# A block-sparse attention feeding a GELU network: shared end-block products moved together, and seven hand-written orders dealt anew

## The chip, the cores and the metric

The kernel runs on one NeuronCore of a Trainium2 chip. The metric is the device time of one execution in microseconds. Three runs of the kernel before took 274.44, 275.01 and 275.5; the median is 275.01. One execution was also recorded by the hardware profiler; every duration, wait and clock in this text comes from that record.

## What is computed

Four batches of eight heads, 768 tokens, 64 numbers a head. Attention looks only at some blocks of 32 tokens: the neighbours, the first and the last block, and three sampled blocks for each of the 24 blocks of queries; the first and the last block of queries see everything. The output, as 3072 tokens of 512 numbers, goes through two matrix products with an exact GELU between.

```python
blk_i, blk_j = pos[:, None] // 32, pos[None, :] // 32
mask = np.abs(blk_i - blk_j) <= 1
mask = mask | (blk_i == 0) | (blk_j == 0) | (blk_i == 23) | (blk_j == 23)
mask[qb * 32:(qb + 1) * 32, kb * 32:(kb + 1) * 32] = True    # three kb for each qb
scores = np.where(mask, np.matmul(q, k.T) / 8, -1e9)
attn = softmax(scores)
x = np.matmul(attn, v)                # (4, 8, 768, 64) -> (3072, 512)
h = x @ w_in                          # 512 -> 2048
out = (0.5 * h * (1 + erf(h / sqrt(2)))) @ w_out
```

## The kernel before

Half a batch is a **unit**: 12 blocks of queries, three *quads* of four. There are eight units; the even ones are *dense* (quads 1, 2, 0) and also do the first and last block of queries of their batch, which see all keys. For each unit the kernel runs FFN1 (first product and GELU, `ffn1_step`, 64 products of 384 columns in eight steps), and then the attention of the *next* unit, with the second product of this unit (FFN2, 48 products of 512 columns) let in between in single pieces by `ffn2_pieces`. Unit 0's attention has nothing to be mixed with but idle products. The attention of unit n is called stage n here; stages 1 to 7 therefore contain FFN2 of the unit before.

The order inside a stage is written by hand as a string of words (`PLANS`, and one string for unit 0), which `attention` (line 600 and on) reads one by one. Each engine executes its instructions in the order in which the words issue them:

- `sN` the score products of round N (`scores`, L346, TensorE, array tile 64x32, into one of two `psA` buffers). A round is two blocks of queries, or one block in the last round of a group of three, or one half of a dense block.
- `mN` its maxima (`maxima`, L372 and L375, VectorE); `eN` its exponentials (L389 and L393, ScalarE), which free the `psA` buffer; `tN` the transpose of 32x32 blocks (L406 and L411, VectorE) into `pT`, which the values products read.
- `wa`, `wb`, `wc` the products with the values for a group (`values`, L470, TensorE); `wd` those of the dense blocks (L433). Groups a and b have four blocks of queries (four *slots*, two rounds each), group c has three. `av` lies in the single `psV` buffer, except for the last group of some units.
- `da`... the division (`divided`, L485 to L489, VectorE); `oa`... the turn to columns (`outputs`, L499, TensorE, with copies on ScalarE), `O` the same with the copy in two parts.
- `fN` N pieces of FFN2 (L566, 128x128 array tile); `S` the pending copy and store of a finished quad (ScalarE, then a store on SP's queue); `G` the load of ScalarE's GELU table.
- `x...` only in stage 1: `xk0` to `xk3` and `xq0` to `xq3` turn one pair of heads of batch 1's keys or queries (`turn_pair`, 16 transposes on TensorE, L234, then one move by ScalarE, or by VectorE with a `d`), `xv` issues the loads of batch 1's values, `xs` repeats the first block of keys.

A slot's values products are eight 32-key chunks c: c = 0 the first block of the sequence, 1 to 3 the neighbours, 4 to 6 the sampled blocks, 7 the last block. Chunks 0 and 7 have the same values for all slots, so for a group with four slots one product with 128 columns of weights serves all four (64x128 array tile, called wide here), where the others take one product with 32 columns for each slot (64x32 tile, narrow). All are done for both heads of a pair (`h`) and both halves of the heads (`G`). The order of the wide products within a group is:

```python
for G in halves:
    work = work + ends if len(halves) == 2 and G else ends + work
```

so a group of four slots issues 4 wide, 48 narrow, 48 narrow and 4 wide products. `start` is set on the first product that writes a slot, for each G anew.

The values of a batch come by eight loads on POOL's queue in the order `VORDER` (`load_values`, L141), heads 0 to 3 first. Keys and queries of batch 1 come by four loads on the same queue behind the weights (`load_kq`, L110), two halves of the heads each; the words `xk` and `xq` use them. Copies of the sampled blocks' keys and values into `gb` (`gather`, L304) run on VectorE and POOL.

Of the kernel before, what the change touches and what calls it, by code (L numbers as in the profile page):

```python
# [20 lines left out]
def kernel(  # L21
# [22 lines left out]
    V2 = 2 * VW  # L44
# [100 lines left out]
    VORDER = sorted(range(H), key=lambda h: (h // 4, (h % 4 ^ h // 4) % 2, h % 4))  # L145
# [273 lines left out]
    def values(unit, grp, halves):  # L419
# [18 lines left out]
        else:  # L438
# [3 lines left out]
            shared = len(slots) == 4  # L442
            for G in halves:
                c0 = KC + V2 * G
                ends = [(0, 4, c, kv[:, blk, c0:c0 + V2]) for c, blk in ((0, 0), (7, NB - 1))] if shared else []
                work = []
                for c in range(1, 7) if shared else range(8):
                    for s, j in enumerate(slots):
# [9 lines left out]
                        work.append((s, 1, c, src))  # L458
                work = work + ends if len(halves) == 2 and G else ends + work
                fresh, left = set(range(len(slots))), {s: 0 for s in range(len(slots))}  # L460
                for s, w, _, _ in work:
                    for x in range(s, s + w):
                        left[x] += 1
                for s, w, c, src in work:
                    at = range(s, s + w)
                    for x in at:
                        left[x] -= 1
                    for h in range(2):
                        rows = slice(64 * h, 64 * h + 64)
                        nc.tensor.matmul(av[32 * s:32 * (s + w), h, V2 * G:V2 * G + V2],  # L470
                                         lhsT=pv[rows, G, c % 4, BL * s:BL * (s + w), c // 4], rhs=src[rows],
                                         start=s in fresh, stop=left[s] == 0)
                    fresh -= set(at)
# [126 lines left out]
    def attention(unit, filler, plan, extra={}, ahead=None):  # L600
# [10 lines left out]
        todo |= {k + c for k in "wdo" for c in groups}  # L611
        for word in plan.split():
            what, arg = word[0], word[1:]
            if what == "s":
                at = [int(i) for i in arg.split("+")]
                scores(rounds[at[0]][0], *[rounds[i][1] for i in at])
                todo -= {f"s{i}" for i in at}
                continue
# [90 lines left out]
    def next_keys(b):  # L709
# [107 lines left out]
```

## Time and profile before

| | us |
|---|---|
| median of three runs | 275.01 |
| the profiled execution | 275.15 |
| its span, first to last instruction | 273.4 |
| TensorE busy | 250.3 |
| VectorE busy | 208.3 |
| ScalarE busy | 206.7 |
| GpSimd busy | 101.7 |

The span is the time between the first and the last recorded instruction; the execution's time has 1.75 us around it. A row of a timeline gives the start, the time until the end of the last of its merged instructions, the engine, the line, what is written from what, the array tile where there is one, and how many instructions were merged; in brackets stands how long the engine had been idle and what released it. Products are pipelined: one of 512 columns lasts 0.38 but the next starts 0.22 after it, and a row may overlap the next one. Some records of products are missing from the trace (an "issue" wait of 0.16 ahead of FFN2 pieces is one such record, not a wait). PEld rows are the weight loads that precede the products.

### The profile page before, as it was taken

The numbers are of one execution on the slowest core, as the hardware profiler recorded it, in microseconds if no ns is written. First come the engines' busy times: TensorE is split into PE (matmuls) and PEld (weight loads), VectorE is DVE, ScalarE is ACT, GpSimd is POOL, SyncE is SP. The second block draws the span as 40 slices with busy tenths as digits, with TensorE's granted clock in tenths as the row PEclk, the third lists the DMA queues.
The fourth block names the chain that finished last, engine by engine and source line by source line (L and its number), as shares of the span: only waits on it lengthen the run. The fifth ranks groups of instructions, "written<-read, shape, count | busy, mean of one in ns | idle before, by whom it ended". The sixth has DMA issues, their size and how long they took to land.

```text
span 273.4 us, 11478 instructions
## 1 busy us (share of the span) xinstructions
PE 250.3 (92%) x4899; PEld 143.7 (53%) x4933; DVE 208.3 (76%) x477; ACT 206.7 (76%) x378; POOL 101.7 (37%) x210
## 2 busy tenths in 40 slices
PE   0798699899999999999999999999999999999995
PEld 0624486355564555545555566455645655465544
DVE  7599969598898989589998987698949996882000
ACT  8679766896868885797868976988788966985611
POOL 7797980717595000950962003910040033000000
PEclk9999689999999999999999999999999999999999
DMA  6999499959999317991997108991101110111002
GB/s 96 183 70 163 75 148 193 206 116 122 63 161 142 102 43 112 114 88 42 120 152 119 62 35 154 89 61 44 40 0 43 43 41 0 38 44 43 0 38 77
DMA packets 73508, 23.80 MB, mean 87 GB/s; under 512 B 63089, under 2 KB 70514, under 8 KB 73458
## 3 DMA queue, kind: packets, MB, share of 16 engines
q0 software_dynamic: 57440, 13.64, 84.4%
q1 hardware_dynamic: 16018, 9.44, 13.6%
q8 instruction: 38, 0.62, 1.0%
q14 instruction: 12, 0.10, 0.1%
HBM read 27.26 MB, written 6.29 MB: 123 GB/s over the span
## 4 chain that ended last, share of the span: by engine, by line
PE 73%; DMA 9%; ACT 6%; DVE 5%; issue 3%; POOL 3%; POOLq 0%; ACTq 0%
PE hp L523 27%; PE op L566 22%; PE av L470 9%; PE sc L346 6%; DMA kn<-in_k_dram 6%; DMA qn<-in_q_dram 3%; PE tx L499 2%; PE op L596 2%; ACT L417 2%; PE pt L234 2%; PE av L433 2%; ACT pp L393 2%; PE av L596 1%; POOL gb L304 1%; ACT pp L389 1%
## 5 line engine op out<-in xcount | busy, mean ns | idle before, releaser
L523 PE MATMUL hp<-xT,w_in_sb 128*128 128x384 bf16 (+2 forms) x536 | 84.9, 319 | 0.2 <-ACT xT L507 0.2
L389 ACT ACTIVATE pp<-sc,nm 128x256 bf16<-128x256 f32 x176 | 74.9, 540 | 7.7 <-DVE nm L372 7.1
L566 PE MATMUL op<-w_out_sb,g 128*128 128x512 bf16 x305 | 75.8, 380 | 4.0 <-issue 3.8
L523 PEld LDWEIGHTS <-w_in_sb 128*128 128x128 bf16 x536 | 51.1, 98 | 33.1 <-issue 0.3
L545 ACT ACTIVATE g<-hp 128x768 bf16<-128x768 f32 x56 | 45.2, 809 | 25.9 <-PE hp L523 25.9
L372 DVE TENSOR_REDUCE nm<-sc 128x4 f32<-128x1024 f32 (+1 forms) x48 | 53.2, 1115 | 6.3 <-PE sc L346 6.0
L566 PEld LDWEIGHTS <-g 128*128 128x128 bf16 x336 | 28.7, 98 | 34.0 <-issue 6.5
L304 POOL COPY gb<-kv 128x388 bf16 (+1 forms) x87 | 36.6, 472 | 23.8 <-DVE gb L295 21.6
L304 DVE COPY gb<-kv 128x388 bf16 x177 | 38.4, 295 | 0.3 <-DVE gb L295 0.2
L406 DVE STREAM_TRANSPOSE pT<-pp 128x512 f32<-128x512 f32 (+1 forms) x48 | 31.4, 657 | 5.3 <-ACT pp L389 4.6
L470 PE MATMUL av<-kv,pT 64*32 64x130 bf16 (+1 forms) x1344 | 30.6, 229 | 1.9 <-DVE pT L406 1.2
L470 PEld LDWEIGHTS <-pT 64*32 64x32 bf16 (+1 forms) x2400 | 26.2, 94 | 10.2 <-DVE pT L406 4.0
L165 POOL COPY mark<-gb 1x1 bf16<-1x1 bf16 x6 | 1.1, 178 | 76.5 <-DVE gb L304 76.5
L141 POOL DMA_DIRECT2D kv<-in_v_dram x32 | 23.0, 726 | 2.5 <-DMA qn<-in_q_dram 1.4
L346 PE MATMUL sc<-gb,qT 64*32 64x256 bf16 x704 | 18.5, 275 | 2.6 <-ACT pp L389 1.8
L507 ACT COPY xT<-tx 128x512 bf16<-128x512 bf16 (+1 forms) x32 | 13.7, 453 | 9.1 <-PE tx L499 9.1
L470 PE MATMUL av<-gb,pT 64*32 64x130 bf16 x1056 | 20.2, 231 | 0.0
L346 PEld LDWEIGHTS <-qT 64*32 64x32 bf16 x832 | 9.3, 90 | 20.4 <-issue 12.3
L417 ACT ACT_TABLE_LOAD x15 | 19.2, 1283 | 0.2
L489 DVE TENSOR_TENSOR xh<-av,rec 128x512 bf16<-128x512 f32 (+2 forms) x28 | 18.2, 652 | 1.0
L393 ACT ACTIVATE pp<-sc,nm 128x768 bf16<-128x768 f32 x16 | 16.7, 1101 | 2.5 <-DVE nm L375 2.2
L550 ACT COPY os<-op 128x512 f32<-128x512 f32 (+1 forms) x23 | 13.1, 570 | 7.0 <-PE op L596 4.3
(79 smaller groups left out, 230.2 us busy)
## 6 DMA issues: line engine op xcount, KB each, us to landing
out_dram<-os SPq DMA_DIRECT2D x23, 256.0 KB, 3.3
kv<-in_v_dram POOLq DMA_DIRECT2D x32, 96.0 KB, 6.6
w_in_sb<-in_moe_w_in_dram POOLq DMA_DIRECT2D x4, 512.0 KB, 7.3
w_out_sb<-in_moe_w_out_dram POOLq DMA_DIRECT2D x2, 1024.0 KB, 12.1
kn<-in_k_dram POOLq DMA_DIRECT2D x4, 384.0 KB, 10.8
qn<-in_q_dram POOLq DMA_DIRECT2D x4, 384.0 KB, 12.2
qn<-in_q_dram POOLq DMA_DIRECT2D x12, 128.0 KB, 5.4
kn<-in_k_dram POOLq DMA_DIRECT2D x12, 128.0 KB, 5.9
```

Source lines behind the costliest of these rows:

```text
L141: nc.gpsimd.dma_start(out=kvs[b % 2][32 * hh:32 * hh + 32, 0:NB, c0:c0 + D], in_=v[b, h].rearrange("(n p) d -> p n d", p=BL))
L304: (engine or nc.vector).tensor_copy(sampled(unit.place[j], r)[:, None, c0:c1], src[:, bass.ds(at[j][r], 1), :])
L346: nc.tensor.matmul(o, lhsT=qT[rows, j // 4, pr, BL * (j % 4):BL * (j % 4) + BL], rhs=rhs(rows, pr), start=True, stop=True)
L372: nc.vector.tensor_reduce(out=nm[:, 0:2 * n].rearrange("p (g j) -> p g j", g=2), in_=A4[:, :, 0:n, :], op=ALU.max, axis=AX.X, negate=True)
L389: nc.scalar.activation(at[:, x // n, x % n], A[:, a:a + 256].rearrange("p (e c k) -> p e c k", e=2, k=BL), AF.Exp, bias=nm[:, x:x + 1])
L393: nc.scalar.activation(pp[:, 0:S].rearrange("p (c k e) -> p c e k", e=2, k=BL), A[:, 0:S].rearrange("p (c e k) -> p c e k", e=2, k=BL), AF ...
L406: nc.vector.transpose(pt.rearrange("p g c x -> p (g c) x")[:, :, 64 * s:64 * (s + n)].bitcast(F32), pp[:, 0:512 * n].bitcast(F32).rearrang ...
L417: nc.scalar.activation(junk, zero[0:1, 0:1], func)
L470: nc.tensor.matmul(av[32 * s:32 * (s + w), h, V2 * G:V2 * G + V2], lhsT=pv[rows, G, c % 4, BL * s:BL * (s + w), c // 4], rhs=src[rows], st ...
L523: nc.tensor.matmul(hp[:, i, c0:c1], lhsT=w_in_sb[:, ki, (m + i) * P:(m + i + 1) * P], rhs=xTs[n % 2][:, ki, c0:c1], start=(ki == 0), stop= ...
L545: nc.scalar.activation(g[:, m:m + 2, 0:T], hp[:, :, 0:T], AF.Gelu)
L566: nc.tensor.matmul(op, lhsT=g[:, m, t * P:(t + 1) * P], rhs=w_out_sb[:, m, :], start=(m == 0), stop=(m == KOUT - 1))
```

## The change

Four things change. The values products of both halves G are collected into one list, the eight wide products of a four-slot group stand together, and they come first, or last where the TensorE word before was a score round or a values block that is not the dense one; `start` is now set once for each slot and not for each half. The heads 4 to 7 of the values are loaded first. In unit 1's order the keys are turned later. The orders of units 2 to 7 are dealt anew.

```diff
-    VORDER = sorted(range(H), key=lambda h: (h // 4, (h % 4 ^ h // 4) % 2, h % 4))
+    VORDER = sorted(range(H), key=lambda h: (-(h // 4), (h % 4 ^ h // 4) % 2, h % 4))
...
-    def values(unit, grp, halves):
+    def values(unit, grp, halves, ends_last=False):
...
+            ends, work = [], []
             for G in halves:
                 c0 = KC + V2 * G
-                ends = [(0, 4, c, kv[:, blk, c0:c0 + V2]) for c, blk in ((0, 0), (7, NB - 1))] if shared else []
-                work = []
+                if shared:
+                    ends += [(G, 0, 4, c, kv[:, blk, c0:c0 + V2]) for c, blk in ((0, 0), (7, NB - 1))]
                 for c in range(1, 7) if shared else range(8):
...
-                        work.append((s, 1, c, src))
-                work = work + ends if len(halves) == 2 and G else ends + work
-                fresh, left = set(range(len(slots))), {s: 0 for s in range(len(slots))}
...
+                        work.append((G, s, 1, c, src))
+            work = work + ends if ends_last else ends + work
+
+            fresh, left = set(range(len(slots))), {s: 0 for s in range(len(slots))}
...
+        tall = False
         for word in plan.split():
             what, arg = word[0], word[1:]
+            if what in "sfwoOx":
+
+                before, tall = tall, what in "sw" and arg[0] != "d"
...
-                values(unit, groups[arg[0]], halves)
+                values(unit, groups[arg[0]], halves, before)
...
     PLANS = {
-        1: ("s0 m0 s1 f12 m1 e0 e1 S xk0d s2 f1 m2 t0 f5 s3 e2 xq0d f5 m3 t1 xk1 t2 e3 s4 m4 f4 xq1 xv wa  "
-            "s5 t3 m5 xk2d f5 e4 s6 f1 da e5 xq2 wb m6 t5 db S xq3 t4 s7 f3 m7 oa f3 xk3d wc f1 e7 e6 ob  "
-            "f4 dc t7 Oc t6 f5 xs G"),
-        2: ("S s1 s0 m1 f3 e1 f6 m0 s2 t1 m2 e0 e2 t0 f7 s3 wd s4 m3 f2 t2 f4 e3 dd m4 od e4 f4 t3 s5 m5  "
-            "wa e5 s6 t4 m6 f6 da f2 s7 m7 e6 e7 S f1 t5 G f5 t6 oa t7 wb wc db f1 dc ob f4 Oc"),
-        3: ("s0 m0 e0 s1 m1 e1 t0 f14 s2 m2 f5 s3 S t1 f2 e2 wa m3 e3 t2 da s5 f3 m5 f4 e5 oa s4 f2 t3 wb  "
-            "m4 f2 e4 t5 f4 db S s6+7 t4 m7 ob wc e7 f8 m6 dc e6 Oc f1 t6 t7 G"),
-        4: ("s0+1 f11 m0 m1 e0 s2 f3 t0 S e1 m2 s3 f2 e2 t1 m3 e3 t2 f1 wd s4 f5 s5 m4 f6 dd f2 e4 t3 m5  "
-            "od s6 wa f1 t4 m6 f1 e5 f1 da s7 e6 m7 f2 e7 t5 f1 t6 oa f4 wb t7 wc f1 G db S ob f4 dc Oc  "
-            "f1"),
-        5: ("s0 m0 s1 m1 e0 f14 e1 t0 s2 f5 m2 s3 f2 t1 m3 f1 wa e2 s5 f4 t2 e3 da S m5 f1 t3 oa s4 m4 f4  "
-            "e5 e4 t5 wb db t4 S f5 s6+7 ob m6 wc f8 e6 m7 dc e7 Oc G f1 t7 t6"),
-        6: ("s0+1 m0 m1 f8 e0 f3 e1 t0 S s2 m2 f3 t1 f1 e2 f3 s3 m3 wd e3 s4 t2 f3 m4 f3 s5 dd f2 m5 f4  "
-            "t3 e4 f1 t4 od s6 wa e5 f2 s7 f2 m6 da f1 m7 t5 f1 e6 f2 t6 f1 e7 t7 oa wb db G wc f1 dc ob  "
-            "f3 S f1 Oc f1"),
-        7: ("s0 m0 e0 s1 f7 m1 e1 f7 t0 s2 m2 f5 t1 s3 m3 f9 e2 t2 S s4 S e3 wa m4 da s5 f4 e4 t3 f6 m5  "
-            "e5 oa t4 t5 wb db wc dc f1 G ob f4 Oc"),
+        1: ("s0 f5 s1 m0 m1 e0 e1 f8 s2 f2 m2 xk0 f1 t0 s3 S f2 xq0d f5 e2 xk1 m3 t1 s4 f3 m4 e3 t3 xq1  "
+            "xv wa s5 da t2 f1 m5 xk2 f5 e4 xq2d wb t4 f2 e5 xq3 db s6 s7 f1 ob f4 S t5 m7 m6 xk3d wc dc  "
+            "e7 e6 oa f2 xs t6 f3 Oc f2 t7 G f3"),
+        2: ("s1 m1 e1 s0 f10 m0 e0 t1 s2 f2 m2 t0 e2 f5 S s3 wd m3 s4 f2 t2 e3 f7 m4 dd e4 s5 t3 od f1 m5  "
+            "wa s6 f2 e5 f6 t4 m6 e6 f1 s7 da m7 t5 f1 t6 S f3 e7 f1 oa t7 wb wc G db ob f4 dc Oc"),
+        3: ("s0 s1 f1 m0 f3 m1 f5 e0 f5 t0 s2 e1 m2 e2 f5 t1 f3 s3 m3 wa da s4 m4 t2 f5 S e3 f1 e4 oa f4  "
+            "t3 s5 m5 e5 wb t4 f4 s6+7 db ob t5 m7 e7 m6 e6 wc f6 dc f2 Oc G t7 S t6 f1"),
+        4: ("s0+1 m0 S m1 e0 f11 s2 e1 t0 f5 m2 e2 s3 t1 m3 e3 t2 f1 wd s4 f5 s5 m4 e4 dd t3 f7 od s6 m5  "
+            "t4 wa e5 m6 da f6 e6 s7 f3 m7 t5 f2 e7 t6 oa G t7 wb wc S db f1 ob f3 dc f1 Oc f1"),
+        5: ("s0 s1 m0 m1 e0 S f14 s2 f1 e1 f4 s3 f3 t0 m2 e2 t1 m3 wa s5 f4 t2 m5 f2 da e3 S t3 s4 e5 oa  "
+            "m4 f4 wb f5 t5 e4 db s6+7 t4 ob m7 m6 wc dc e7 e6 t6 f7 Oc G f1 t7"),
+        6: ("s0+1 S f4 m0 e0 f6 m1 f1 e1 s2 t0 f5 m2 s3 e2 f1 t1 wd m3 s4 t2 e3 f7 m4 e4 s5 dd m5 f6 s6  "
+            "t3 f2 e5 S m6 wa t4 s7 e6 f5 da m7 od e7 f3 t5 t6 oa wb t7 wc db f1 G dc ob f4 Oc f1"),
+        7: ("s0 s1 f9 m0 e0 f1 m1 t0 f5 e1 s2 f4 m2 t1 s3 f8 m3 e2 e3 t2 f1 s4 f1 m4 wa e4 S s5 f5 t3 m5  "
+            "f4 e5 da oa t4 wb G t5 wc db f1 dc ob f4 S Oc"),
     }
```

Unit 0's order is not changed, but its values blocks take the new form: `wa` follows a score round and has its wide products last, `wb` has them first.

More of the change, by code (lines that the diff above doesn't have):

```diff
@@ L457, in values @@
                             src = sampled(unit.place[j], c - 4)[:, c0:c0 + V2]
-                        work.append((s, 1, c, src))
-                work = work + ends if len(halves) == 2 and G else ends + work
-                fresh, left = set(range(len(slots))), {s: 0 for s in range(len(slots))}
[L461 to L473, printed above, removed]
+                        work.append((G, s, 1, c, src))
+            work = work + ends if ends_last else ends + work
+            fresh, left = set(range(len(slots))), {s: 0 for s in range(len(slots))}
+            for G, s, w, _, _ in work:
+                for x in range(s, s + w):
+                    left[x] += 1
+            for G, s, w, c, src in work:
+                at = range(s, s + w)
+                for x in at:
+                    left[x] -= 1
+                for h in range(2):
+                    rows = slice(64 * h, 64 * h + 64)
+                    nc.tensor.matmul(av[32 * s:32 * (s + w), h, V2 * G:V2 * G + V2],
+                                     lhsT=pv[rows, G, c % 4, BL * s:BL * (s + w), c // 4], rhs=src[rows],
+                                     start=s in fresh, stop=left[s] == 0)
+                fresh -= set(at)
             n, m = len(slots), 4
```

## The prediction

> **What bounds the kernel now.** I read the page's busy table first, then busy time by stretch (cut at the FFN1 blocks), then TensorE's waits, then TensorE's timeline in single stages.
>
> ```profile
> span 273.4 us, 11478 instructions
> PE 250.3 (92%) x4899; PEld 143.7 (53%) x4933; DVE 208.3 (76%) x477; ACT 206.7 (76%) x378; POOL 101.7 (37%) x210
> ```
>
> ```profile
> 0.00:38.50 38.50, 26.22 (x688) 15.78 (x691) 30.54 (x70) 30.04 (x47) 33.07 (x89) 0.91 1.67 120
> 48.40:72.20 23.80, 21.80 (x588) 12.31 (x593) 19.32 (x31) 18.85 (x39) 11.85 (x29) 1.00 1.71 134
> 82.70:103.50 20.80, 19.37 (x560) 10.94 (x564) 18.34 (x34) 17.50 (x38) 3.31 (x8) 1.00 0.72 89
> 114.00:131.90 17.90, 17.10 (x461) 9.09 (x466) 15.60 (x25) 15.73 (x34) 8.66 (x16) 1.00 1.83 65
> 142.40:162.20 19.80, 19.00 (x559) 10.54 (x563) 17.49 (x31) 17.44 (x37) 2.89 (x7) 1.00 0.47 79
> 172.70:190.60 17.90, 17.11 (x460) 9.01 (x465) 15.42 (x25) 15.78 (x35) 6.00 (x12) 1.00 1.70 63
> 201.10:221.30 20.20, 19.34 (x559) 10.86 (x563) 17.69 (x31) 17.38 (x38) 0.69 (x2) 1.00 0.08 29
> 231.80:249.00 17.20, 16.52 (x445) 9.21 (x449) 13.17 (x21) 15.01 (x34) 0.00 (x0) 1.00 0.09 34
> ```
>
> Columns: stretch, length, busy us of TensorE (PE), its weight loads, VectorE (DVE), ScalarE (ACT), GpSimd (POOL), granted clock. The first row is unit 0's attention, the others are the attention stages of units 1 to 7, whose orders are rewritten; the FFN1 blocks between them are not touched. In stages 1 to 7 TensorE is busy 92 to 97% of the time, but VectorE and ScalarE are at 77 to 88% as well: two engines stand close behind the one that bounds.
>
> ```profile
> PE sc L346 <- ACT pp L389: 1.8, 3, 0.9
> PE pt L234 <- DMA kn<-in_k_dram: 1.6, 2, 0.9
> PE av L470 <- DVE pT L406: 1.2, 1, 1.2
> PE av L470 <- issue: 0.5, 1, 0.5
> ```
>
> These are nearly all the waits of TensorE behind the start-up. The 0.9 is the key transpose in stage 1; the 1.2 is in unit 0; the 0.5 is a stall inside one values block of stage 2 with no releaser. So TensorE's length in stages 2 to 7 is its own work plus what it loses where it changes from one kind of work to another.
>
> **The hand-overs.** Stage 3, once with FFN2 pieces on both sides, once between two score rounds in stage 2:
>
> ```profile
> 123.98 0.60 PE L566 MATMUL op<-w_out_sb,g 128*128 128x512 bf16 x2
> 124.52 0.58 PE L470 MATMUL av<-kv,pT 64*128 64x130 bf16 x28
> ...
> 125.12 0.42 PE L470 MATMUL av<-kv,pT 64*32 64x130 bf16 x24
> 125.32 0.42 PE L470 MATMUL av<-gb,pT 64*32 64x130 bf16 x24
> 125.67 0.29 PE L470 MATMUL av<-kv,pT 64*128 64x130 bf16 x4
> 125.89 0.55 PEld L566 LDWEIGHTS <-g 128*128 128x128 bf16 x4
> ...
> 92.50 0.41 PE L346 MATMUL sc<-gb,qT 64*32 64x256 bf16 x16
> 92.85 0.58 PE L470 MATMUL av<-kv,pT 64*128 64x130 bf16 x28
> 94.00 0.29 PE L470 MATMUL av<-kv,pT 64*128 64x130 bf16 x4
> 94.22 0.41 PE L346 MATMUL sc<-gb,qT 64*32 64x256 bf16 x16
> ```
>
> 24 narrow products (64x32 array tile) start within 0.20 us. The last 24 begin at 125.32, so they are through at 125.52; the four wide ones (64x128 tile) start at 125.67. That gap, 0.15, is the price of a change of array tile. The block takes 1.37 either way (124.52 to 125.89, 92.85 to 94.22): 0.80 of narrow products, the rest eight wide ones and three hand-overs.
>
> **The change part by part.** *Values.* The same 104 products of a four-slot block run as 8 wide + 96 narrow, or 96 narrow + 8 wide where the last TensorE word was a score round or another values block. One hand-over inside goes, and another where the narrow end meets narrow score rounds or the narrow `wc`. The before shows no score round directly followed by narrow products: bounds 0.01 (same tile, pitch of the narrow products) and 0.15 (as between any two tiles); I take 0.01, since both use the 64x32 tile. The Trainium skill (TensorEngine Tiling, Key Properties) says that a change of tiling mode drains the array, a change of tile within a mode does not; the 0.15 agrees with the first half, no pair here shows the second; by it the 0.01 holds.
>
> Counted from the order strings, stage by stage (1 to 7), changes of array tile: before 29, 20, 20, 22, 20, 21, 16 = 148; after 30, 17, 14, 18, 17, 18, 13 = 127. (With the old orders and new values it would be 123, so the new orders themselves win none.) 21 × 0.15 = 3.15 us of TensorE time; bounds 0 and 3.15.
>
> How much of it arrives depends on VectorE. In unit 3 the new order puts round 4's maxima and both transposes behind the division of group a: da, m4, t2, t3, and then `wb`, which needs t3.
>
> ```profile
> 118.33 1.19 DVE L372 TENSOR_REDUCE nm<-sc 128x4 f32<-128x1024 f32 x1
> 119.44 0.69 DVE L406 STREAM_TRANSPOSE pT<-pp 128x512 f32<-128x512 f32 x1
> 120.05 1.18 DVE L372 TENSOR_REDUCE nm<-sc 128x4 f32<-128x1024 f32 x1
> ...
> 121.95 0.13 DVE L485 TENSOR_SCALAR den<-av 128x8 f32<-128x8 f32 x1
> ...
> 122.95 0.68 DVE L372 TENSOR_REDUCE nm<-sc 128x2 f32<-128x512 f32 x1
> ...
> 114.78 2.97 PE L566 MATMUL op<-w_out_sb,g 128*128 128x512 bf16 x13 [0.16 <-issue]
> ```
>
> Start to start: maximum 1.11, transpose 0.61, division 1.00 (121.95 to 122.95). From the end of `wa`: 1.00 + 1.11 + 0.61 + 0.69 = 3.4, plus 0.1 until the division sees the sums and 0.1 to the products: 3.6. TensorE meanwhile has s4 (0.35), ten FFN2 products at 0.216 ((2.97 − 0.38)/12) = 2.16, oa (0.2), s5 and its hand-overs (0.2): 2.9. So `wb` waits some 0.7, which eats most of that stage's six hand-overs (0.9): −0.2 there. In the other stages I find no such reversal against the order before (units 2 and 7: t3 ahead of m5), but TensorE, being earlier, meets operands that VectorE, at 77 to 88%, delivers no earlier. Of the other 15 hand-overs (2.25) I let a little over half arrive: −1.3. Sum **−1.5**.
>
> *Later keys in unit 1.*
>
> ```profile
> 37.59 15.22 DMA kn<-in_k_dram
> 48.44 0.63 PE L346 MATMUL sc<-gb,qT 64*32 64x256 bf16 x32
> 49.01 2.93 PE L566 MATMUL op<-w_out_sb,g 128*128 128x512 bf16 x11
> 52.86 0.53 PE L234 MATMUL pt<-identity,kn 96*64 96x96 bf16 x16 [0.93 <-DMA kn<-in_k_dram]
> ```
>
> The keys land at 37.59 + 15.22 = 52.81. TensorE was through at 51.94, and could have started 0.16 earlier (a product lasts 0.38, its successor starts after 0.216): lost 1.1. The new order puts 15 FFN2 products ahead instead of 12 (0.65) and round 2's scores (0.35, as 92.50 to 92.85 above, and a hand-over, 0.1): 1.1 later, just when the keys are there. They land no earlier; queued behind the waiting transpose were s2 and with it VectorE's next maximum. Stage 1's hand-overs are up by one. Gain between 0 (another wait takes its place, such as s3 for the exponentials) and 1.1; I take **−0.9**, as the cover is exact and leaves a little over.
>
> *Unit 0* keeps its order but takes the new blocks.
>
> ```profile
> 33.17 0.85 PE L470 MATMUL av<-kv,pT 64*128 64x130 bf16 x28 [1.18 <-DVE pT L406]
> ...
> 34.94 0.40 PE L470 MATMUL av<-kv,pT 64*128 64x130 bf16 x4
> 35.27 0.61 PE L499 MATMUL tx<-identity,xh 128*128 128x128 bf16 x4
> ```
>
> `wb` is released by a transpose at 33.17; what follows (35.27: oa, wc, and FFN1) hangs on it. The clock is lower in unit 0 (0.91 over the stretch above); its last hand-over and four products (34.94 to 35.27, 0.33) shrink to some 0.1 for four more wide products: −0.2. `wa` has the wait of `wb` behind it, so little of its gain passes. **−0.25**, bounds 0 and −0.4.
>
> *V order.* Same eight loads, same bytes, one queue; gathers take both halves' columns, so they wait for the last load whatever the order.
>
> ```profile
> 63.32 3.53 POOL L141 DMA_DIRECT2D kv<-in_v_dram x5 [0.20 <-issue]
> 76.12 7.10 DVE L304 COPY gb<-kv 128x388 bf16 x25 [0.22 <-DVE gb L295]
> kv<-in_v_dram POOLq DMA_DIRECT2D x32, 96.0 KB, 6.6
> ```
>
> The last is issued by 66.9 and lands 6.6 later, 73.5; the gathers begin at 76.1. The cover is 2.6 us; 0, bounds ±0.3 for unit 0, where less covers it. The stall without releaser (0.5) stays; bounds: gone, or one more.
>
> **Sum.** −1.5 − 0.9 − 0.25 = −2.65. The profiled execution took 275.15 (span 273.4 and 1.75 around it), 0.14 above the median 275.01. Against the median: 275.01 − 2.65 = **272.4**, its own range 271.4 to 273.6.
>
> **Rivals.**
> 1. *All of TensorE's saving arrives.* For: stages 3 and 5 hold no TensorE wait worth naming before, so an order that keeps operands ahead passes it on. Against: `wb` in unit 3. 275.01 − 3.15 − 1.1 − 0.4 = 270.4.
> 2. *VectorE sets the pace in stages 2 to 7*, the hand-overs give nothing and TensorE idles instead. For: 17.5 to 18.3 us busy in stages of 20. Against: it still has 2 us there. Only keys and unit 0 remain: 275.01 − 1.15 = 273.9, up to 275.6 if they fail too. The Trainium skill (TensorEngine Tiling, PSUM Bottleneck) warns of this: tiling speeds up TensorE, not the evacuation, which can become the bottleneck; by that rule this case; the rows show VectorE near, not at, its limit.
> 3. *Slower: maxima ahead of transposes.* At the value blocks of units 2 to 7 TensorE waits for a transpose that stands behind a maximum more (1.11). Unhidden in all six stages: 6 × 1.11 = 6.7, less 3.15 + 1.1 + 0.25: +2.2, 277.2. It decides above (4.5/6) 0.75 us of new wait per stage; unit 3's 0.7 is near that, the others show no such place.
>
> **How the numbers follow.** Forecast 0.45, rival 1 0.20, rival 2 0.22, rival 3 0.13. About 0.5% (1.4 us) is what a measurement here can tell from no change. Faster by more (below 273.6): the forecast, rival 1 and a sliver of rival 2: 0.66; within it, the rest of rival 2 and a bit of rival 3: 0.22; slower 0.12. The range takes in the forecast, rival 1 with 0.4 for the unknown costs, and rival 2 up to 275.4: 270.0 to 275.4, leaving out most of rival 3.
>
> **What would show it.** Values blocks: first wide row x8, no second wide row, 0.15 less each. Stage 1 shorter by 0.9 with the wait for kn gone; if another TensorE wait near 53 to 55 us has its place, that step is wrong. Stage 3 about as long as before, with TensorE waiting for a pT at `wb`; no wait there and 17.0 us would be rival 1. Stages 2, 4 to 7 shorter by 0.2 to 0.4 each; unchanged with more TensorE idle for VectorE is rival 2; longer, rival 3.

## The result, and the profile after

The kernel is slower. Against the kernel before on the same chip (275.42 us, median of 22 runs) it takes 278.77 (median of 22): a ratio of 1.0096, interval 1.0067 to 1.0126. The forecast was 272.4, in a range of 270.0 to 275.4. Run again beside other kernels it took 278.26 (ratio 1.0079, 1.0045 to 1.0113). The profile below is a recorded execution from that second series: 278.75, span 276.9.

```profile
span 276.9 us, 11516 instructions
PE 254.4 (92%) x4933; PEld 144.7 (52%) x4933; DVE 206.0 (74%) x476; ACT 207.3 (75%) x379; POOL 101.8 (37%) x210
```

Busy shares hardly differ from before, so they don't tell where 3.5 us of span came from. The stages do. The rows are cut at the first and the last product of each FFN1 block, so that nothing falls between them but FFN1 itself (columns as in the prediction's table; behind the clock stand the packet times of all DMA transfers added up, as a share of the 16 DMA engines, and GB/s):

```profile
0.00:38.57 38.57, 24.41 (x675) 15.01 (x676) 28.84 (x68) 29.44 (x46) 32.31 (x87) 0.94 1.55 117
50.13:73.77 23.64, 22.59 (x594) 12.11 (x593) 18.76 (x30) 19.55 (x40) 14.33 (x31) 1.00 1.74 132
85.06:105.45 20.39, 19.94 (x566) 10.91 (x564) 17.59 (x31) 17.59 (x38) 2.21 (x5) 1.00 0.35 68
115.69:134.01 18.32, 17.94 (x467) 9.29 (x465) 15.98 (x26) 15.91 (x35) 9.04 (x17) 1.00 1.60 66
144.25:165.51 21.26, 19.91 (x565) 10.87 (x564) 17.86 (x33) 17.81 (x38) 2.89 (x7) 1.00 0.53 75
175.74:194.14 18.40, 18.16 (x468) 9.01 (x465) 15.40 (x25) 16.02 (x35) 6.32 (x13) 1.00 1.55 63
204.38:224.50 20.12, 19.84 (x564) 10.64 (x563) 17.43 (x31) 17.61 (x38) 0.99 (x3) 1.00 0.08 29
234.74:252.60 17.86, 17.46 (x451) 9.10 (x449) 13.16 (x21) 15.53 (x34) 0.00 (x0) 1.00 0.09 33
```

The gaps between the rows are the FFN1 blocks: the first takes 50.13 − 38.57 = 11.56, the second 85.06 − 73.77 = 11.29, all others 10.24 or less than 0.02 from it. With the kernel before cut in the same way, and three kernels of the experiments beside it:

| us | before | after | changed kernel, old load order | before, new load order | changed kernel, old load order, heads aligned |
|---|---|---|---|---|---|
| unit 0 | 37.31 | 38.57 | 36.36 | 37.70 | 37.25 |
| its granted clock | 0.91 | 0.94 | 1.00 | 1.00 | 0.94 |
| FFN1 of unit 0 | 10.88 | 11.56 | 10.86 | 10.86 | 11.52 |
| stage 1 | 24.02 | 23.64 | 24.26 | 25.77 | 22.73 |
| FFN1 of unit 1 | 10.24 | 11.29 | 10.24 | 10.24 | 10.24 |
| stage 2 | 21.04 | 20.38 | 20.38 | 20.65 | 20.41 |
| stage 3 | 18.14 | 18.32 | 18.11 | 18.53 | 18.12 |
| stage 4 | 20.11 | 21.26 | 20.90 | 20.27 | 20.56 |
| stage 5 | 18.16 | 18.40 | 18.41 | 18.15 | 18.16 |
| stage 6 | 20.47 | 20.13 | 20.12 | 20.21 | 20.13 |
| stage 7 | 17.48 | 17.86 | 17.87 | 17.99 | 17.29 |

Unit 0 and its FFN1 carry some 1 to 2 us of noise between executions of one kernel: the granted clock dips there by different amounts, and differences of those rows below that size are read with their clock only. TensorE's waits in the kernel after:

```profile
PE av L472 <- DVE pT L406: 1.9, 2, 1.6
...
PE pt L234 <- DMA qn<-in_q_dram: 1.5, 1, 1.5
PE op L568 <- issue: 1.2, 1, 1.2
...
PE av L472 <- POOL gb L304: 1.0, 1, 1.0
PE hp L525 <- issue: 0.9, 1, 0.9
PE pt L234 <- issue: 0.8, 1, 0.8
PE pt L234 <- DMA kn<-in_k_dram: 0.4, 1, 0.4
```

The wait for batch 1's keys (0.9 in stage 1) is gone; the 0.4 is the start-up's. In its stead there are three waits that nothing releases ("issue"), 2.9 together, where the kernel before had two, of 0.5 and 0.4; and the queries of batch 0 are waited for 1.5 instead of 0.6. Neither stood in the sum.

### The profile page after: what moved, and what is told of

Its sections match the earlier page's. It is cut to its first block, busy times and chain, and to the rows that moved or that the text cites. A ratio compares the mean times of both kernels' runs of the same rounds, so it can differ in the third digit from the quotient of the medians.

```text
span 278.8 us, 11516 instructions
## 1 busy us (share of the span) xinstructions
PE 254.7 (91%) x4933; PEld 143.0 (51%) x4933; DVE 206.6 (74%) x476; ACT 207.5 (74%) x379; POOL 101.6 (36%) x210
## 3 DMA queue, kind: packets, MB, share of 16 engines
q0 software_dynamic: 57440, 13.64, 81.2%
## 4 chain that ended last, share of the span: by engine, by line
PE 67%; DMA 10%; DVE 8%; ACT 7%; POOL 4%; issue 3%; POOLq 1%; ACTq 0%
PE hp L525 27%; PE op L568 21%; PE av L472 7%; PE sc L346 4%; DMA kv<-in_v_dram 4%; DMA ptd<-kn 3%; DMA qn<-in_q_dram 3%; POOL gb L304 3%; DVE nm L372 3%; PE tx L501 2%; ACT pp L389 2%; PE op L598 2%; ACT L417 2%; PE pt L234 1%; DVE pT L406 1%
## 5 line engine op out<-in xcount | busy, mean ns | idle before, releaser
L568 PE MATMUL op<-w_out_sb,g 128*128 128x512 bf16 x336 | 85.6, 387 | 0.4 <-ACT kv L251 0.2
L372 DVE TENSOR_REDUCE nm<-sc 128x4 f32<-128x1024 f32 (+1 forms) x48 | 54.1, 1168 | 8.9 <-PE sc L346 8.6
L304 DVE COPY gb<-kv 128x388 bf16 x177 | 36.8, 288 | 0.5 <-DMA qn<-in_q_dram 0.5
L472 PEld LDWEIGHTS <-pT 64*32 64x32 bf16 (+1 forms) x2400 | 25.5, 91 | 10.8 <-DVE pT L406 4.3
L472 PE MATMUL av<-kv,pT 64*32 64x130 bf16 (+1 forms) x1344 | 27.7, 221 | 3.3 <-DVE pT L406 1.9
L375 DVE TENSOR_REDUCE nm<-sc 128x1 f32<-128x768 f32 x16 | 14.7, 949 | 7.0 <-PE sc L346 6.9
```

The lines of the kernel that those rows point to most:

```text
L304: (engine or nc.vector).tensor_copy(sampled(unit.place[j], r)[:, None, c0:c1], src[:, bass.ds(at[j][r], 1), :])
L372: nc.vector.tensor_reduce(out=nm[:, 0:2 * n].rearrange("p (g j) -> p g j", g=2), in_=A4[:, :, 0:n, :], op=ALU.max, axis=AX.X, negate=True)
L568: nc.tensor.matmul(op, lhsT=g[:, m, t * P:(t + 1) * P], rhs=w_out_sb[:, m, :], start=(m == 0), stop=(m == KOUT - 1))
```

## The experiments

Times are medians; a ratio is that of the kernel to the kernel before on the same chip, with its 95% interval (it need not be the quotient of the two medians). Most rows rest on 10 to 12 runs; those of heads 1 3 0 2 and of 66 columns rest on 6. The kernel before took 275.62 beside the first four runs, 275.47, 275.12 and 275.30 beside the next three groups of four. "Changed kernel" is the kernel after.

| run | median us | ratio | interval |
|---|---|---|---|
| changed kernel again | 278.26 | 1.0079 | 1.0045 to 1.0113 |
| changed kernel, old load order | 274.37 | 0.9958 | 0.9923 to 0.9992 |
| before, new load order | 277.65 | 1.0083 | 1.0049 to 1.0118 |
| before, new values blocks only | 275.28 | 0.9989 | 0.9956 to 1.0023 |
| changed kernel, heads 4 6 5 7 1 3 0 2 | 275.05 | 0.9988 | 0.9959 to 1.0018 |
| changed kernel, heads 1 3 0 2 4 6 5 7 | 279.18 | 1.0106 | 1.0059 to 1.0153 |
| new values, old load order, new order for unit 1 only | 274.42 | 0.9977 | 0.9951 to 1.0003 |
| the same, new orders for units 2 to 7 only | 274.96 | 0.9982 | 0.9952 to 1.0012 |
| changed kernel, 66 columns a head | 278.47 | 1.0118 | 1.0083 to 1.0153 |
| the same, old load order | 278.59 | 1.0138 | 1.0099 to 1.0177 |
| changed kernel, old load order, batch 1's values not loaded | 273.26 | one run | |
| changed kernel, old load order, t2 and t3 moved up in unit 3 | 276.0 | 1.0024 | 0.9994 to 1.0054 |
| changed kernel, heads aligned | 274.40 | 0.9966 | 0.9929 to 1.0003 |
| the same, old load order | 273.66 | 0.9955 | 0.9920 to 0.9989 |
| before, heads aligned | 274.27 | 0.9987 | 0.9958 to 1.0015 |
| new values, order of unit 1, old load order, heads aligned | 273.65 | 0.9954 | 0.9927 to 0.9981 |

**The change taken apart.** First the changed kernel as it is, then with the old order of V's loads, then the kernel before with only the new order of loads, then the new values blocks alone.

> The changed kernel unaltered, for a second trace. Two things cost most in its first trace: in stage 3 the repeat of the first key block on VectorE (L272) took 3.28 us beside GpSimd's copies and TensorE waited 2.8 us, and in stage 1 TensorE stood still for 0.96 and 1.22 us inside dense stretches with no releaser. Theory orders (the new orders and blocks cause both): both are there again, time 278 to 279. Theory V order (heads 4 to 7 first make loads and the key transpose land late, by chance of the moment): stage 3's loss may be absent, then about 276; the stalls of stage 1 stay.

```diff
-    VORDER = sorted(range(H), key=lambda h: (-(h // 4), (h % 4 ^ h // 4) % 2, h % 4))
+    VORDER = sorted(range(H), key=lambda h: (h // 4, (h % 4 ^ h // 4) % 2, h % 4))
```

> The changed kernel with the old order of the values' loads. Theory V order: the first load lands within 3.5 us of its issue as before (4.6 in the changed kernel), the keys' transpose for batch 2 lands 6.9 us after its issue instead of 8.5, stage 3 back to 17.9 us, 2.5 to 4 us faster than the changed kernel, below the kernel before. Theory orders: within 0.8 us of the changed kernel.

> The kernel before with heads 4 to 7 loaded first and nothing else. Theory V order: 1 to 3 us slower than the kernel before, with stage 3 longer. Theory orders: the same within 0.7 us.

> The new values blocks alone: old orders, old order of loads. By the count of changes of array tile (148 to 123, 0.15 us each) 3.7 us at most, by the half that I let arrive 1.5 to 2 us faster than the kernel before. If denser narrow stretches bring more stalls without releaser (rival), no gain or 1 us slower, with such stalls inside wa to wc.

One line of the diff carries the loss. Without it the changed kernel takes 274.37, 1.2 below the kernel before; with it alone the kernel before takes 277.65, 2.0 more than without. The values blocks alone give 0.3 us, which the interval doesn't tell from nothing, where 1.5 to 2 were expected. The loss in stage 3 of the first trace did not come again (18.32 instead of 22.56), and yet the time stayed at 278.26, not near 276. The clock doesn't make the difference: among the executions with a mean granted clock of at least 0.999 the changed kernel's median is 277.9 (10 of its 33), and 274.9 with the old load order (6 of 12).

**Which property of the order?** The new order differs from the old in two ways. It takes heads 4 to 7 first; and, because of the `^ h // 4` in the key, it starts with odd heads (5 7 4 6 0 2 1 3), where the old started with even ones (0 2 1 3 5 7 4 6). Two more orders take the two apart.

```diff
+    VORDER = [4, 6, 5, 7, 1, 3, 0, 2]
...
+    VORDER = [1, 3, 0, 2, 4, 6, 5, 7]
```

> The changed kernel with the values' loads in the order 4 6 5 7 1 3 0 2. In the runs so far the order 5 7 4 6 0 2 1 3 lands its first load 4.6 to 4.9 us after issue and the last 12.1 to 14.3 after, the order 0 2 1 3 5 7 4 6 2.8 to 3.4 and 11.2 to 12.2. Theory parity: odd heads, whose rows are written at an odd multiple of 2 bytes (columns of 65 numbers), land slowly, and it matters that they do not stand first; then the first load lands near 3 us here and the time is that of the old order, 274.4. Theory halves: heads 4 to 7 ahead of 0 to 3 are what costs; then first landing near 4.7 and 278.

> The changed kernel with the values' loads in the order 1 3 0 2 4 6 5 7. Theory parity: first landing near 4.7 us, time near 278. Theory halves: first landing near 3 us, time 274.4.

It is the parity: heads 4 to 7 first with an even head in front costs 0.7 by the medians (275.05 against 274.37, the intervals overlap), heads 0 to 3 with an odd one in front costs as much as the change (279.18). A head's values have 65 columns of two bytes, the 64 values and a one, and two heads stand side by side; so the second one, the odd head, begins at an odd column, at no multiple of four bytes. The timelines show the first place where it is felt: the last of the four key and query loads of batch 0, just ahead of the values on the same queue. The same product in the kernel before, in it with the new load order, in the changed kernel, in it with the old load order, with 4 6 5 7 first and with 1 3 0 2 first, one fence for each:

```profile
12.59 0.85 PE L234 MATMUL pt<-identity,qn 96*64 96x96 bf16 x16 [0.59 <-DMA qn<-in_q_dram]
```

```profile
12.62 0.85 PE L234 MATMUL pt<-identity,qn 96*64 96x96 bf16 x16 [1.19 <-DMA qn<-in_q_dram]
```

```profile
12.88 0.85 PE L234 MATMUL pt<-identity,qn 96*64 96x96 bf16 x16 [1.48 <-DMA qn<-in_q_dram]
```

```profile
11.91 0.85 PE L234 MATMUL pt<-identity,qn 96*64 96x96 bf16 x16 [0.53 <-DMA qn<-in_q_dram]
```

```profile
11.99 0.85 PE L234 MATMUL pt<-identity,qn 96*64 96x96 bf16 x16 [0.53 <-DMA qn<-in_q_dram]
```

```profile
13.35 0.85 PE L234 MATMUL pt<-identity,qn 96*64 96x96 bf16 x16 [1.90 <-DMA qn<-in_q_dram]
```

0.5 to 0.6 with an even head behind the queries, 1.2 to 1.9 with an odd one. (One further trace with an even head there, that of unit 3's other order below, shows 0.97, so the wait varies by itself too.) The eight loads of a batch share the 16 DMA engines with what was issued just before and after them. Slow packets in front delay the load that is about to end; slow packets at the back delay only loads that are waited for later. The wait for the queries is 0.6 to 1.4 us longer with the odd head, and unit 0 ends later by about as much: 37.66 and 37.70 where its clock was 1.00, against 36.36 to 37.12 in the six traces of the same layout and clock with an even head in front. Another part is in waits of stage 1 and the FFN1 behind it, which come below: 1.5 to 2.3 us together in the four traces with an odd head in front, 0.3 to 1.3 in those with an even one. What is left of the 2.0 to 3.9 us is not located. Over all 32 loads of V, the shortest, median and longest time from issue to landing show the same in the kernel before and in the changed kernel: the median is no different, but no load is quick any more.

```profile
DMA to landing us min/median/max: 2.9/6.6/11.3
```

```profile
DMA to landing us min/median/max: 4.6/6.6/12.5
```

**Is it the odd column?** First attempt: 66 columns a head, so that no head begins at an odd column.

```diff
-    VW = D + 1
+    VW = D + 2
```

> The changed kernel (loads in the order 5 7 4 6 0 2 1 3) with 66 columns a head in the values tiles instead of 65 (one unused), so that every head's rows begin at a multiple of 4 bytes. Theory parity (an odd multiple of 2 bytes makes a write slow): the first load lands near 3 us after issue instead of 4.6 to 4.9, and the time falls from 278.3 to 275 or less; products of 132 columns instead of 130 cost at most 1.5% of the 51 us of narrow products, 0.8. Rival (something else of the odd heads, such as their place in HBM): first landing stays near 4.7, time 278 to 279.

> The same 66 columns with the old order of loads 0 2 1 3 5 7 4 6. Theory parity: with no slow heads left the order is nothing, the same time as the run before within 0.7 us, the last load lands earlier than 11.5 us, and less of the other transfers' time is lost: 273.5 to 275. Rival: as the 65-column kernel with that order, 274.4, plus up to 0.8.

The loads became fast (3.7 us to landing instead of 6.6) and both load orders took the same time, but both over 3 us more than the kernel before. In unit 0 a wait appears that neither kernel had, here with the old load order. The mean granted clock was lower too (0.98 over these runs, 1.00 over those of the kernel before), and how the loss divides between the two stays open:

```profile
30.41 0.30 PE L346 MATMUL sc<-gb,qT 64*32 64x256 bf16 x8 [1.99 <-POOL gb L304]
```

So a second layout keeps the 130 columns of a pair and puts the two ones behind the 128 values. No head begins at an odd column (the offsets are multiples of 4 bytes, not of 32), and the stride of a block is as before. `divided` reads accordingly, and takes no longer: its first instruction 0.154 us and its last 0.652 on average, as without the layout.

```diff
-        c0 = KC + V2 * G + VW * (hh % 2)
+        c0 = KC + V2 * G + D * (hh % 2)
...
-                c0 = KC + V2 * G + VW * (hh % 2 ^ G) + D
+                c0 = KC + V2 * G + 2 * D + (hh % 2 ^ G)
...
-        a = av[rows, :, 0:VW * m].rearrange("p h (x d) -> p h x d", d=VW)
+        a = av[rows, :, 0:VW * m].rearrange("p h (g c) -> p h g c", c=V2)
```

> The changed kernel with its load order, but the two heads of a pair of values stand side by side (columns 0 to 63 and 64 to 127) and their two columns of ones behind them: still 130 columns a pair, no head begins at an odd column any more, and the column stride of the blocks is that of before. Alignment theory (what costs is the load of a head into rows that begin at an odd number of 2-byte columns, and odd heads first put that ahead of batch 1's queries): the first load lands about 3.0 us after its issue and the last by 9, the attention of unit 0 takes 36.4 to 36.9 (the changed kernel: 37.7 to 39.0), no wait of scores for a gather in unit 0, 273.0 to 274.5. Rival 1 (the order of the halves or of the heads itself costs, whatever the columns): 278, as the changed kernel. Rival 2 (what made the 66-column layout slow is any other layout of the pairs): unit 0 takes 40 to 41, 278 to 279.

> The same layout with the load order of before. Alignment theory: no more than 0.8 us from the run with the new load order, 273.0 to 274.5; the changed kernel without the layout had 3.9 us between the two orders. Rival 1: 274.4, that is 3.5 to 4 us less than with the new load order. Rival 2: 278 to 279.

> The kernel before with this layout alone. Alignment theory: V's loads land 2.5 to 3 us sooner in each batch (last 9 us after the first issue instead of 11.7), which the old orders use little; stalls of TensorE without releaser in stage 1 below 0.5 together; 274.0 to 275.2 against 275.4. If instruction blocks wait for other traffic than V's, the stalls stay and the time is within 0.5 of before.

> The layout with the new values blocks, unit 1's new order, the old orders of units 2 to 7 and the old load order, which without the layout took 274.4. Alignment theory: stage 1 loses the 0.5 us of stalls it still had there, 273.3 to 274.3, the fastest of all or level with the other two. If the layout gives nothing where even heads are loaded first: 274.4.

The cost of the load order falls from 278.26 − 274.37 = 3.9 us to 274.40 − 273.66 = 0.7. The queue, the median load and the product that waits for the queries, with the aligned heads and the new load order:

```profile
q0 software_dynamic: 57440, 13.64, 53.5%
...
kv<-in_v_dram POOLq DMA_DIRECT2D x32, 96.0 KB, 3.7
```

```profile
11.97 0.85 PE L234 MATMUL pt<-identity,qn 96*64 96x96 bf16 x16 [0.53 <-DMA qn<-in_q_dram]
```

In the kernel before the same row of the queues reads:

```profile
q0 software_dynamic: 57440, 13.64, 84.4%
```

The same 57440 packets and 13.64 MB take 53.5% of sixteen engines' 274.3 us instead of 84.4% of 273.4: 41 ns a packet instead of 64. Packet by packet the traces say it more plainly. Of the 49152 packets of 128 bytes on this queue 12288 are rows of odd heads (four batches, four heads, 768 rows); 11663 took 40 ns or more in the kernel before, 523 with the aligned heads (new load order), and the median is 32 ns in both. A load of one head lands after 3.7 instead of 6.6. Alignment is shown to be what makes the loads slow, and the load order to cost little without it (0.7, which the intervals don't tell from nothing). The kernel before gains 1 us by it in the medians and 0.1% in the ratio, within its interval; with even heads in front its wait for the queries was short already (0.59). One detail of the expectations failed: the recorded execution with the new load order, the slowest of its twelve (276.13), took 37.51 in unit 0 and not 36.4 to 36.9, with a wait of 1.90 without a releaser in it, of the kind that follows.

**The waits that nothing releases.** One run issues no loads of batch 1's values.

```diff
             elif word == "xv":
-                load_values(1)
```

> The changed kernel with the old order of loads, and batch 1's values not loaded at all (its columns stay zero, so batch 1's output is not the reference's). If the stalls of stage 1 at the instruction-block borders (TensorE instructions 2240, 2496, 2752; 0.4 and 0.9 us in that kernel) come from blocks that queue behind the values' loads, they are gone and stage 1 is 1 to 1.4 us shorter. Rival (the dense stretches alone outrun the fetch, whatever else moves): the stalls stay.

The last five products of a key transpose in stage 1 stand behind such a wait in most kernels. Before, before with the new load order, the changed kernel, and it with the old load order:

```profile
68.53 0.29 PE L234 MATMUL pt<-identity,kn 96*64 96x96 bf16 x5 [0.35 <-issue]
```

```profile
70.65 0.29 PE L234 MATMUL pt<-identity,kn 96*64 96x96 bf16 x5 [1.49 <-issue]
```

```profile
70.08 0.29 PE L234 MATMUL pt<-identity,kn 96*64 96x96 bf16 x5 [0.78 <-issue]
...
77.10 3.09 PE L525 MATMUL hp<-xT,w_in_sb 128*128 128x384 bf16 x18 [0.89 <-issue]
```

```profile
67.78 0.29 PE L234 MATMUL pt<-identity,kn 96*64 96x96 bf16 x5 [0.74 <-issue]
```

Without batch 1's loads this wait is gone, in the one execution there is, and stage 1 is 23.15 instead of 24.26. With aligned heads and the new load order it is 0.15, with the old one none is left. With 66 columns, where the loads are as fast, it was 0.90 with the old load order and absent with the new; so fast loads alone don't remove it, and its size differs from kernel to kernel, one execution each. What TensorE waits for is its own code: in the changed kernel's trace, where all its instructions are recorded, the breaks fall at instructions 1216 (in unit 0), 2496, 2752, 5824 and 9152, all apart by multiples of 256, and the queue table has a queue for code with 38 transfers in 0.62 MB, 16 KB each:

```profile
q8 instruction: 38, 0.62, 1.0%
```

The Trainium skill (Runtime: NRT & Kernel Launch, Instruction fetch mechanics) says that each engine's code is refilled in blocks of 16 KiB, 256 instructions, which these numbers agree with; it also says that the cost of crossing such a border is mostly hidden, which does not hold at these. The trace has the 38 transfers one by one, and they settle it. TensorE stands at instruction 5824 from 156.38 on; a transfer of this queue runs from 155.11 to 156.31, and the next product starts at 157.76. Over all 18 traces, TensorE's waits of 0.2 us and more behind 30 us that have no releaser, with those at instruction 1216, are 63; 61 of them end 1.1 to 2.1 us after the end of such a transfer. The block came late.

V's loads are not the only thing that makes it late. The waits at 5824 (stage 4) and 9152 (stage 7) stayed without batch 1's loads (0.7 and 0.5 between two starts of TensorE), and in stage 7 the DMA engines have little to do (a share of 0.09 in the last row of the table of stages). In the changed kernel TensorE crosses the border before 9152 at 240.38; the next transfer starts 1.4 later and takes 1.7, and TensorE goes on 1.5 after its end: 4.6 us, where it had run through the 256 instructions in 4.0. So here the rival of that expectation holds, a dense stretch outruns the fetch. What decides when a transfer starts was not tried.

**The hand-overs.** The new orders in two halves, and unit 3 with its transposes ahead of the division and the maximum, so that `wb` needn't wait.

```diff
-        3: ("s0 s1 f1 m0 f3 m1 f5 e0 f5 t0 s2 e1 m2 e2 f5 t1 f3 s3 m3 wa da s4 m4 t2 f5 S e3 f1 e4 oa f4  "
-            "t3 s5 m5 e5 wb t4 f4 s6+7 db ob t5 m7 e7 m6 e6 wc f6 dc f2 Oc G t7 S t6 f1"),
+        3: ("s0 s1 f1 m0 f3 m1 f5 e0 f5 t0 s2 e1 m2 e2 f5 t1 f3 s3 m3 wa t2 da s4 f5 S e3 f1 oa f4 t3  "
+            "m4 e4 s5 m5 e5 wb t4 f4 s6+7 db ob t5 m7 e7 m6 e6 wc f6 dc f2 Oc G t7 S t6 f1"),
```

> Old orders with new values blocks and old order of loads, and unit 1's new order alone. My sum: the wait of 1.1 us for the keys goes, 0.9 us faster than the same kernel with unit 1's old order (275.28), so 274.4. Rival: instruction-block stalls (at every 256th TensorE instruction, 2240, 2496, 2752, while the values are being loaded) take the place: stage 1 not shorter, 275.3.

> New values blocks, old order of loads, unit 1's old order and units 2 to 7's new ones. If the new orders 2 to 7 give nothing beyond the blocks (they win no change of tile, and unit 3 waits 0.6 us at wb): 275.3 as with all old orders. If they do help: 274.3 or less.

> The changed kernel with the old order of loads, and in unit 3's order the transposes t2 and t3 ahead of the division's successor m4 (wa t2 da s4 ... t3 m4 e4). My step: wb waits 0.6 us for t3 behind da, m4, t2; with t3 ahead of m4 the wait at TensorE instruction 4575 (0.58) goes, and stage 3 (18.1 between the FFN1 blocks) gets 0.3 to 0.6 shorter. Rival: VectorE's work is the same, the wait turns up later in the stage (wc or Oc), length unchanged.

Stage 3 of the changed kernel, the values block between two score rounds and the start of `wb`:

```profile
121.84 0.41 PE L346 MATMUL sc<-gb,qT 64*32 64x256 bf16 x16
122.07 0.42 PE L472 MATMUL av<-kv,pT 64*32 64x130 bf16 x24
122.28 0.43 PE L472 MATMUL av<-gb,pT 64*32 64x130 bf16 x24
122.49 0.42 PE L472 MATMUL av<-kv,pT 64*32 64x130 bf16 x24
122.69 0.42 PE L472 MATMUL av<-gb,pT 64*32 64x130 bf16 x24
123.04 0.40 PE L472 MATMUL av<-kv,pT 64*128 64x130 bf16 x8
123.37 0.41 PE L346 MATMUL sc<-gb,qT 64*32 64x256 bf16 x16
...
126.43 0.23 PE L472 MATMUL av<-kv,pT 64*32 64x130 bf16 x4
127.01 0.35 PE L472 MATMUL av<-kv,pT 64*32 64x130 bf16 x20 [0.35 <-DVE pT L406]
```

The new block works as it was meant to. Score round and block take 123.37 − 121.84 = 1.53, before 94.22 − 92.50 = 1.72: 0.19 less, where the sum had two hand-overs, 0.30. Narrow products follow a score round 0.23 after its start, while a wide block took 0.35; at the end of the narrow ones there is the gap of 0.15 as before (122.69 + 0.20 to 123.04). By the starts of the single products, 0.11 is saved at the end of the score round and 0.15 inside, and 0.07 is lost again, as the wide and narrow products themselves take that much longer. Beside the values alone (275.28), the new orders of units 2 to 7 give 274.96, that of unit 1 274.42, both 274.37; these steps are within the intervals. Moving unit 3's transposes up was worse: stage 3 took 19.29 instead of 18.11, with the waits now ahead of a score round and of the turn to columns:

```profile
127.83 0.37 PE L346 MATMUL sc<-kv,qT 64*32 64x512 bf16 x1 [0.19 <-ACT pp L389]
128.61 0.52 PE L346 MATMUL sc<-kv,qT 64*32 64x512 bf16 x15 [0.41 <-DVE den L487]
129.59 0.40 PE L501 MATMUL tx<-identity,xh 128*128 128x128 bf16 x4 [0.46 <-DVE xh L491]
```

Why does a saved hand-over not shorten the stage? The old orders with the new blocks show it in stage 3, where nothing else differs. Round 6+7, which follows the second block, starts 13.01 after the stage's first score round (112.82) instead of 13.30 (113.99): the two blocks have saved 0.29. The rows around it, with the new blocks and in the kernel before:

```profile
125.08 0.93 ACT L389 ACTIVATE pp<-sc,nm 128x256 bf16<-128x256 f32 x2
...
125.83 0.74 PE L346 MATMUL sc<-kv,qT 64*32 64x512 bf16 x16
...
126.51 0.40 PE L501 MATMUL tx<-identity,xh 128*128 128x128 bf16 x4
```

```profile
126.63 0.54 ACT L389 ACTIVATE pp<-sc,nm 128x256 bf16<-128x256 f32 x1
...
127.29 0.52 PE L346 MATMUL sc<-kv,qT 64*32 64x512 bf16 x16
...
127.74 0.40 PE L499 MATMUL tx<-identity,xh 128*128 128x128 bf16 x4
```

With the new blocks the round starts at 125.83, while ScalarE's exponentials, which free the second `psA` buffer, last until 125.08 + 0.93 = 126.01; it takes 0.68 until the next product (126.51). Before, it started at 127.29, after their end at 127.17, and took 0.45. So 0.23 of the 0.29 is given back here, to a wait for the exponentials. The merged row hides it; in the trace the second of the sixteen products starts 0.23 after the first (before: 0.004), at 126.06, 0.05 after the exponentials' end, and has them as its releaser. The stage comes out at 18.08 instead of 18.14.

Other savings went into the waits for code. In the changed kernel with the old load order, stages 4, 5 and 7 are longer than before by 0.79, 0.25 and 0.39, and each holds one such wait, of 0.81, 0.23 and 0.38; without these they would be as long as before, not shorter. Behind unit 0 these waits (of 0.2 us and more) add up to 0.9 us in the kernel before, 1.3 with the new values blocks alone, 2.4 in the changed kernel with the old load order and 3.4 in the changed kernel, one execution each.

## Why the prediction was wrong

**The step that failed: "V order ... 0, bounds ±0.3".** It measured +2.0 us in the kernel before (277.65 against 275.62) and +3.9 in the changed one (278.26 against 274.37). "Same eight loads, same bytes, one queue" was right and did not suffice: the eight loads are not alike, and which of them comes first decides what they delay. The step looked only at the last load and at who waits for it. It did not ask what else is in flight beside the first ones (the queries of batch 0, the code blocks in stage 1), nor whether a head's rows begin alike. That every second head begins at an odd column could be read in `load_v`. Rival 3 alone had a slower kernel, 277.2, but that the result lies near it is luck: what it feared, waits for a transpose in units 2 to 7, is 0.3 us in the changed kernel (1.9 in the list above, of which 1.6 is in unit 0).

**Hand-overs, −1.5: mis-sized.** The price holds where it was taken: 0.15 between narrow and wide, and close to nothing between a score round and a narrow product of the same tile (0.09 from the round's last start to the first narrow one, where the round's own two groups of eight products lie 0.10 apart). The rule in the Trainium skill (TensorEngine Tiling (Array Packing), Key Properties) that only a change of mode drains the array, of which the trace before showed one half, is borne out in the other by the row at 122.07. But at 0.19 for 0.30 a block is worth less than the count, and little arrives. The new values blocks alone gave −0.3 us (0.9989, 0.9956 to 1.0023). Stages 3 to 6 together went from 76.88 to 76.77 with them. This is the second rival in part, TensorE meeting the other engines' operands, though it was ScalarE's exponentials at one place that showed it and not VectorE; the waits for code are the other part, which no rival had. Rival 2's "up to 275.6 if they fail too" does not follow from its own sum, which gives 275.0. The "little over half" was argued from busy shares, and these say nothing about slack at a given wait.

**Later keys in unit 1, −0.9: right, and then given back.** No wait for the keys is left in stage 1, as the order was read. Where the code stalls are small, stage 1 comes out at 23.01 (heads 4 6 5 7 first) and 23.21 (unit 1's order alone), 22.73 with the aligned heads: 0.8 to 1.3 below 24.02. (In the first two the FFN1 behind the stage is 0.5 longer, by a wait for code that has moved there.) In the changed kernel with the old load order, whose stage 1 has the stall of 0.74 and shorter ones, it is 24.26. The prediction named another TensorE wait near 53 to 55 us as the sign of failure; the wait that came stands at 70, without a releaser.

**Unit 0, −0.25: not seen.** The six traces with the new blocks, an even head in front and a clock of 1.00 spread from 36.36 to 37.12, more than the term. The step "what follows hangs on it" was wrong: behind group b, group c stands again, at instruction 1216. The list above puts this wait (1.0) down to POOL's copies of sampled blocks, and they do end just before; but in every trace except the kernel before's it ends 1.1 to 1.5 us after the end of a code transfer, and with the aligned heads and the new load order the last copy had ended 1.2 us earlier. An earlier group b moves nothing past that. In the kernel before's trace the clock was 0.5 from 29.5 to 36.4, and the wait did not show.

**Unit 3's wait for t3, 0.7: right.** TensorE stood 0.58 at `wb` (126.43 to 127.01), and the stage was not shorter, as forecast.

**"The stall without releaser stays; bounds: gone, or one more"** took as a detail what became most of the loss in stage 4 (1.15 longer, with a wait of 1.17) and in the FFN1 behind stage 1 (1.05 longer, with one of 0.89). The trace before held two such waits behind the start-up, that of 0.5 in stage 2 and the 0.35 at 68.53 in stage 1, which the list of "nearly all the waits" left out; both end 1.3 to 1.8 us after a code transfer. The 0.5 in stage 2 went in the changed kernel and accounts for most of that stage's 0.66.

Without the load order, the change is worth 0.4% (0.9958, 0.9923 to 0.9992): 1.2 us, less than half of the 2.65. The two fastest kernels, both below the kernel before by their intervals, have the aligned heads and the old load order: 273.66 with all new orders, 273.65 with unit 1's alone.

## What to carry to other kernels

When loads are reordered, look at each load's own time to landing and not at the sum of the bytes, and name everything that shares the DMA engines with the first one as well as with the last. Pack rows so that each transfer begins at a multiple of four bytes in on-chip memory; a column of ones belongs behind the pair, not between its two halves. A saving on the busiest engine is only a saving if the next buffer it needs is already free: follow each one to the next wait before it goes into a sum. And a wait without a releaser is worth its instruction number: if such waits lie apart by multiples of 256 and end behind the transfers of the code queue, TensorE has outrun its own code, and a denser order brings more of them.

## What was not expected of the hardware

Rows of 128 bytes that begin at an odd 2-byte column cost much more to write: 64 ns against 41 for a packet, over all packets of the queue, of which only half of V's are affected. And one recorded execution of the changed kernel, the first (280.66), held something that came in no other trace. A copy of 128 columns on VectorE took 3.28 us, beside copies on GpSimd that began 0.47 after it:

```profile
116.41 3.28 DVE L272 COPY kv<-kv 128x128 bf16<-128x128 bf16 x1
116.70 2.99 DVE L372 TENSOR_REDUCE nm<-sc 128x4 f32<-128x1024 f32 x2
116.88 4.12 POOL L304 COPY gb<-kv 128x388 bf16 x9
```

In the second trace the same copy took 0.20:

```profile
115.42 0.20 DVE L272 COPY kv<-kv 128x128 bf16<-128x128 bf16 x1
```

That execution's stage 3 was some 4 us longer (22.56 instead of 18.32). By way of the two maxima and the exponentials behind it TensorE stood for 2.77 (until 121.51); and from 121.8 to 125.2 its granted clock was 0.5, with FFN2 products 0.42 apart instead of 0.22, which is about the rest. What made the copy slow was not provoked again and is open.
